# Where a row block's statistics and a shared bank's copies are computed: five tiles moved to VectorE, six copies to ScalarE

## The chip, the cores and the metric

The kernel runs on one core of a Trainium2 chip. The metric is the device time of one execution in microseconds. The kernel before was run five times; its median is 1464.83 us (1460.11 to 1469.95).

## The reference

The reference is an adaptive-layernorm block. A vector c gives six modulation rows; x goes through a layernorm with modulation and a recurrent attention over segments of 32 tokens, and then through a shifted mixer with an MLP. The change touches only the second half of the mixer:

```python
        hs = jnp.concatenate([g0, g1, g2, g3], axis=-1) @ w2
        x1 = x + hs
        h2 = _gelu(_layernorm(x1, axis=-1) @ w3) @ w4
        return x1 + h2
```

Here x has 2048 rows of 1024, w2 is 1024 x 1024, w3 is 1024 x 3584 and w4 is 3584 x 1024, all in bf16. The layernorm subtracts a row's mean and divides by the root of its variance plus 1e-5.

## The kernel before, in words

The kernel first does the attention (its projections, scores and outputs take most of the span), then the mixer in three stages: w1 (lines 1225 to 1233), w2 (lines 1355 to 1386) and w3 with w4 (lines 1430 to 1588). w1's last tiles end at about 1048.5 us of the profiled execution, w2 lasts until 1104.1, and w3 and w4 take the rest.

**w2.** The 2048 rows are worked in 16 tiles of 128 rows, t0 to t15. `Ba(t)` (line 1355) loads the tile u (what is added to the product) with a DMA on SP's queue, and multiplies two halves of 512 columns by eight matmuls each (line 1366), each half in a PSUM bank of its own. VectorE adds u while it takes a half out of its bank into x1b (line 1368, an operation that also sums each row), and ScalarE's queue stores x1b to memory (line 1369). Then comes `ln_sums` (line 1340), the layernorm of the tile: VectorE makes the negative mean of the two row sums (lines 1343, 1344), ScalarE squares x1b minus the mean and sums the squares of each row (line 1346, into z, which is overwritten later), GpSimd makes the factor and the offset in three small operations (lines 1348, 1350, 1352), and ScalarE applies them, giving z in bf16 (line 1353). `Bb(t)` (line 1374) turns z by a DMA transpose, issued on SP, into z2s, where w3 reads it. `lagged` runs `Bb(t-1)` ahead of `Ba(t)`.

The order on each engine's queue is the program's, fitted by the framework's scheduler. Three things tie the tiles together. The accumulators come from eight banks in turn, but from t13 on from the four banks of `psB` alone (line 1378). The pools of z and x1b hold four tiles each, so that t15's z lies where t11's was, and writing it waits until t11's transpose has landed. And between the tiles, seven sums of w3 weights and of z (`w3_sums` and `z_sums`, all line 1292) are put on VectorE at steps 6 to 13 (line 1385); the sums of z need the transposes of t0 to t7.

**w3.** `w3_stage(pair)` (line 1430) works on half of the rows at a time, in seven groups of columns, by a Strassen-Winograd scheme with seven products per group (line 1447). In each group, for each of two halves q: the first product goes into `bank_b`, and is copied out by `snap` (lines 1407 and 1461) while the bank goes on collecting; the second goes into `bank_e`, and `join` (line 1455) adds the copy to it on VectorE, after which ScalarE applies gelu (line 1451); the third goes into `bank_d`, copied out at line 1470; the fourth is added in `bank_b`, copied out at line 1472; then the fifth, named S3 in the code, is added in `bank_b`, the sixth, S4, in `bank_d`, and the seventh in `bank_b` again. A product that adds to a bank waits until the copy of what stood there is done. The banks are opened anew for w3, over those of w2: `bank_e` and `bank_d` lie where `psB` was. The w3 loop is under `manual_schedule`, so its order is written out by hand. In the very first group (n == 0) the six copies are made by VectorE (line 1410), in the other 13 by ScalarE (line 1412). Then w4 (`w4_stage`) follows, and both again for the second half of the rows.

Of the kernel before, what the change touches and what calls it, by code (L numbers as in the profile page):

```python
# [10 lines left out]
F32 = mybir.dt.float32  # L11
F16 = mybir.dt.float16
I32 = mybir.dt.int32
ACT = mybir.ActivationFunctionType
ALU = mybir.AluOpType
# [4 lines left out]
P = 128  # L20
# [9 lines left out]
NTT = S // P  # L30
# [30 lines left out]
def kernel(ctx, tc, A_x, A_mem0, A_Wq, A_Wk, A_Wv, A_Wo, A_seg_len, B_x, B_w1, B_w2, B_w3, B_w4, c, w_mod, out,  # L61
           dbg=None, force_fallback=False, no_fallback=False):
    nc = tc.nc
# [106 lines left out]
    def first_pass(late_hook):  # L170
# [6 lines left out]
        def acc_tile():  # L177
            acc_ctr[0] += 1
            return acc_pools[acc_ctr[0] % len(acc_pools)].tile([P, 512], F32, name="acc")
# [335 lines left out]
        for p in range(2):  # L515
# [3 lines left out]
            s1 = nc.vector.tensor_tensor(S1, A21, A22, ALU.add)  # L519
# [534 lines left out]
        bsm = LT.enter_context(tc.tile_pool(name="x1_sm", bufs=8))  # L1054
# [65 lines left out]
        ln = {}  # L1120

        def ln_stats(t, halves, rstd):
            stt = bsm.tile([P, 2, 6], F32, name="ln_st")
            for i in range(2):
                nc.vector.bn_stats(out=stt[:, i, :], in_=halves[i])
            mv = bsm.tile([P, 2], F32, name="ln_mv")
            nc.vector.bn_aggr(out=mv[:], in_=stt[:])
            nc.vector.tensor_scalar(mv[:, 1:2], mv[:, 1:2], EPS, None, ALU.add)
            nc.vector.tensor_scalar(mv[:, 0:1], mv[:, 0:1], -1.0, None, ALU.mult)
            nmr = bsm.tile([P, 1], F32, name="ln_nmr")  # L1130
            nc.gpsimd.tensor_tensor(rstd, mv[:, 1:2], mhalf[:], ALU.pow)
            nc.gpsimd.tensor_tensor(nmr[:], mv[:, 0:1], rstd, ALU.mult)
            ln[t] = nmr[:], rstd

        def halves_of(ap):
            return [ap[:, n * 512:(n + 1) * 512] for n in range(2)]
# [62 lines left out]
        U1, sums1, _ = wave(1)  # L1199
# [109 lines left out]
        def load_upto(n):  # L1309
            while ring_ctr[0] <= min(n, 21):  # L1310
                ring_load(ring_ctr[0])
                ring_ctr[0] += 1
# [25 lines left out]
        bsm = LT2.enter_context(tc.tile_pool(name="x2_sm", bufs=8))  # L1338

        def ln_sums(smp, dst, src, sums):  # L1340

            nm = smp.tile([P, 1], F32, name="ln_nm")
            nc.vector.tensor_tensor(nm[:], sums[:, 0:1], sums[:, 1:2], ALU.add)
            nc.vector.tensor_scalar(nm[:], nm[:], -1.0 / D, None, ALU.mult)
            sq = smp.tile([P, 1], F32, name="ln_sq")
            nc.scalar.activation(dst, src, ACT.Square, bias=nm[:], accum_out=sq[:])
            ve = smp.tile([P, 1], F32, name="ln_ve")
            nc.gpsimd.tensor_scalar(ve[:], sq[:], 1.0 / D, EPS, ALU.mult, ALU.add)
            rstd = smp.tile([P, 1], F32, name="ln_rstd")
            nc.gpsimd.tensor_tensor(rstd[:], ve[:], mhalf[:], ALU.pow)  # L1350
            nmr = smp.tile([P, 1], F32, name="ln_nmr")
            nc.gpsimd.tensor_tensor(nmr[:], nm[:], rstd[:], ALU.mult)
            nc.scalar.activation(dst, src, ACT.Identity, bias=nmr[:], scale=rstd[:])

        def Ba(t):
            def f():
                ts = slice(t * P, (t + 1) * P)
                u = tu.tile([P, D], BF16, name="u2")
                nc.sync.dma_start(u[:], u_d[ts, :])
                x1b = tp.tile([P, D], F32, name="x1b")  # L1360
                sums = bsm.tile([P, 2], F32, name="ln_sums")
                for n2 in range(2):
                    acc = acc_tile()
                    for kt in range(KT):
                        o = 2 + t * P + SHIFT[kt]
                        nc.tensor.matmul(acc[:], lhsT=h1Ts[kt // 4][:, kt % 4, o:o + P], rhs=w2s[0][:, kt, n2 * 512:(n2 + 1) * 512], start=(kt == 0), stop=(kt == KT - 1))  # L1366
                    cs = slice(n2 * 512, (n2 + 1) * 512)
                    nc.vector.scalar_tensor_tensor(x1b[:, cs], acc[:], 1.0, u[:, cs], ALU.mult, ALU.add, accum_out=sums[:, n2:n2 + 1])
                nc.scalar.dma_start(x1b_d[ts, :], x1b[:])
                zs[t] = z = tz.tile([P, D], BF16, name="z")  # L1370
                ln_sums(bsm, z[:], x1b[:], sums)
            return f

        def Bb(t):
# [24 lines left out]
        stA = RF.enter_context(tc.tile_pool(name="x3_sA", bufs=4, side="right"))  # L1399
        st2 = RF.enter_context(tc.tile_pool(name="x3_s2", bufs=2, side="right"))  # L1400
# [3 lines left out]
        pse = RF.enter_context(tc.tile_pool(name="ps_e", bufs=2, space=PSUM))  # L1404
        psd = RF.enter_context(tc.tile_pool(name="ps_d", bufs=2, space=PSUM))

        def snap(pool, src, on_dve=False):
            s = pool.tile([P, 512], F32, name="snap")
            if on_dve:
                nc.vector.tensor_copy(s[:], src[:])  # L1410
            else:
                nc.scalar.copy(s[:], src[:])  # L1412
            return s

        def addend_units(pair):

            def mk(t, n):
                def f():
                    rows, cs = slice(t * P, (t + 1) * P), slice(n * 512, (n + 1) * 512)
                    xb = rsq.tile([P, 512], F32, name="xb3")  # L1420
                    nc.sync.dma_start(xb[:], x1b_d[rows, cs])
                    x1 = rsq.tile([P, 512], F32, name="x13")
                    nc.sync.dma_start(x1[:], x1_d[rows, cs])
                    nc.gpsimd.tensor_tensor(xb[:], xb[:], gb_b[:, cs], ALU.mult)
                    nc.gpsimd.tensor_tensor(x1[:], xb[:], x1[:], ALU.add)
                    nc.gpsimd.dma_start(rs_d[rows, cs], x1[:])
                return f
            return [mk(t, n) for t in range(pair * 8, pair * 8 + 8) for n in range(2)]

        def w3_stage(pair):  # L1430

            hq = [[hq_p.tile([P, 14, 512], BF16, name=f"hq{a}{f}") for f in range(2)] for a in range(2)]
            A11, A12, S4, A22, S1, S2, S3 = zsum[pair]
            add = addend_units(pair)
            for g in range(7):
                n = pair * 11 + g
                load_upto(n + 2)
                B11, B21, B22, T4, T1, T2, T3 = ready[n]  # L1440
                st = [{} for _ in range(2)]

                def prod(bank, A, B, start):
                    for q in range(2):
                        acc = st[q][bank]
                        for k in range(4):
                            nc.tensor.matmul(acc[:], lhsT=B[:, k, q * P:(q + 1) * P], rhs=A[:, k, :], start=(start and k == 0), stop=(k == 3), skip_group_check=True)  # L1447
                        yield q

                def gelu(a, f, q, src):  # L1450
                    nc.scalar.activation(hq[a][f][:, g * 2 + q, :], src[:], ACT.Gelu_apprx_tanh)  # L1451

                def join(a, f, q, bank, s):
                    t = stm.tile([P, 512], F32, name="join")
                    nc.vector.tensor_tensor(t[:], st[q][bank][:], st[q][s][:], ALU.add)  # L1455
                    gelu(a, f, q, t)

                for q in range(2):
                    st[q]["b"] = psb.tile([P, 512], F32, name="bank_b")
                for q in prod("b", A11, B11, True):  # L1460
                    st[q]["s1"] = snap(stA, st[q]["b"], n == 0)
                for q in range(2):
                    st[q]["e"] = pse.tile([P, 512], F32, name="bank_e")
                for q in prod("e", A12, B21, True):
                    join(0, 0, q, "e", "s1")
                dve(T4, B21, T2, ALU.subtract)
                for q in range(2):
                    st[q]["d"] = psd.tile([P, 512], F32, name="bank_d")
                for q in prod("d", S1, T1, True):
                    st[q]["s5"] = snap(stA, st[q]["d"], n == 0)  # L1470
                for q in prod("b", S2, T2, False):
                    st[q]["s2"] = snap(st2, st[q]["b"], n == 0)
                for q in prod("b", S3, T3, False):
                    join(1, 1, q, "b", "s5")
                for q in prod("d", S4, B22, False):
                    join(0, 1, q, "d", "s2")
                for q in prod("b", A22, T4, False):
                    gelu(1, 0, q, st[q]["b"])
                for u in w3_sums(n + 1) if g < 6 else []:
                    u()  # L1480
                for u in add[16 * g // 7:16 * (g + 1) // 7]:
                    u()
            return hq
# [805 lines left out]
```

## Time and profile before

| What | Value |
|---|---|
| median of five runs | 1464.83 us |
| the profiled execution | 1464.35 us |
| its span, first to last instruction | 1462.6 us |
| TensorE (PE) busy | 1397.9 us, 96% |
| VectorE (DVE) busy | 971.3 us, 66% |
| ScalarE (ACT) busy | 692.1 us, 47% |
| GpSimd (POOL) busy | 480.3 us, 33% |
| mean granted TensorE clock | 0.992 |
| chain that ended last, by engine | TensorE 73%, VectorE 10%, DMA 9%, ScalarE 4% |

How to read it: times are those of one execution. A line of a timeline has the start in us from the span's start, the time it took, the engine, the line of the kernel, the operation, what it wrote and read, the shapes, how many instructions were merged into the line, and in brackets how long the engine sat idle just before and what ended that. In a table of stretches each row has the stretch, its length, and the busy time and count of TensorE's matmuls and weight loads, VectorE, ScalarE and GpSimd; the last three columns are the granted clock as a share of full speed, the busy share of the DMA engines and what they moved in GB/s. Of merged matmuls the time runs to the modelled end of the last one, so neighbours overlap a little; a product of eight matmuls follows the one before at 1.73 us.

### The profile page before, as it was taken

To read this page: it belongs to the slowest core of one execution; us is meant where nothing else is said; L and a number is where in the kernel's file an instruction comes from. 1 tells how busy PE (TensorE), PEld (TensorE's weight loads), DVE (VectorE), ACT (ScalarE), POOL (GpSimd) and SP (SyncE) were. 2 spreads that over 40 slices of the span, in tenths; PEclk is the share of its full clock that TensorE was granted. 3 is DMA by queue.
4 is the path that set the end of the run, shared out by engine and by line. 5 is a ranking of instruction groups with operands and counts; after the bars stand their busy time and mean duration, and the time that the engine had idled before them with its cause. 6 is when DMAs were issued, how large, how long until landed. Compare 5 with 4: busy or idle time off the path is not lost.

```text
span 1462.6 us, 24721 instructions
## 1 busy us (share of the span) xinstructions
PE 1397.9 (96%) x9080; PEld 741.4 (51%) x9126; DVE 971.3 (66%) x1995; ACT 692.1 (47%) x1473; POOL 480.3 (33%) x661
## 2 busy tenths in 40 slices
PE   6999999999999999999999999999797999999998
PEld 4665555555555555555555444444343444444443
DVE  6627777777776778777754648887255667566684
ACT  3635566465665656566664013326365650056400
POOL 6120321514122202220001025555124663546625
PEclk9999999999999999999999999999999999999999
DMA  9778978878787776787749999969499783477812
GB/s 336 271 227 197 183 169 201 210 162 211 177 196 201 171 173 162 182 201 182 161 135 315 356 374 288 309 189 262 137 273 224 237 280 109 151 230 250 283 40 79
DMA packets 389237, 310.69 MB, mean 212 GB/s; under 512 B 199658, under 2 KB 336874, under 8 KB 385266
## 3 DMA queue, kind: packets, MB, share of 16 engines
q1 hardware_dynamic: 356576, 244.03, 62.0%
q0 software_dynamic: 13856, 46.16, 9.0%
q10 hardware_dynamic: 18674, 18.83, 4.3%
q8 instruction: 73, 1.20, 0.3%
q14 instruction: 58, 0.48, 0.1%
HBM read 199.38 MB, written 59.02 MB: 177 GB/s over the span
## 4 chain that ended last, share of the span: by engine, by line
PE 73%; DVE 10%; DMA 9%; ACT 4%; issue 3%; POOL 1%; SPq 0%; ACTq 0%; DVEq 0%; POOLq 0%
PE acc L649 26%; PE acc L987 9%; PE bank_b L1498 7%; PE bank_b L1447 6%; PE acc L323 3%; PE bank_d L1447 3%; DMA s<-OTw_d 3%; PE bank_e L1498 2%; PE bank_d L1498 2%; PE acc L333 2%; PE acc L1366 2%; PE ps_o L774 2%; DMA wk<-in_A_Wk_dram 2%; PE ps_s L757 2%; PE bank_e L1447 1%
## 5 line engine op out<-in xcount | busy, mean ns | idle before, releaser
L649 PEld LDWEIGHTS <-T 128*128 128x128 f16 x1408 | 130.7, 98 | 124.6 <-issue 9.9
L617 ACT COPY snap<-acc 128x480 f32<-128x480 f32 x264 | 146.0, 565 | 91.3 <-PE acc L649 81.3
L987 PE MATMUL acc<-wstream,s 128*128 128x512 f16 (+1 forms) x855 | 187.0, 379 | 1.7 <-DMA wstream<-in_A_Wo_dram 0.6
L649 PE MATMUL acc<-hs,T 128*128 128x480 f16 x704 | 160.5, 367 | 5.1 <-DVE QT L621 2.9
L649 PE MATMUL acc<-hh,T 128*128 128x480 bf16 (+1 forms) x704 | 163.8, 368 | 1.1 <-DVE KT L621 0.9
L987 PEld LDWEIGHTS <-s 128*128 128x128 f16 (+1 forms) x864 | 84.3, 98 | 103.9 <-DVE s L1002 1.8
L1447 PEld LDWEIGHTS <-ring 128*128 128x128 f16 (+1 forms) x784 | 77.0, 98 | 104.9 <-issue 13.3
L799 POOL DMA_DIRECT2D OTw_d<-OT x32 | 24.7, 773 | 264.0 <-DMA OT<-O 217.4
L761 ACT ACTIVATE E<-ps_s 99x495 bf16<-99x495 f32 (+2 forms) x160 | 88.0, 550 | 41.4 <-PE ps_s L757 41.0
L649 PE MATMUL acc<-hh,wq 128*128 128x480 bf16 x464 | 105.5, 365 | 0.0
L781 DVE TENSOR_TENSOR O<-ps_o,rin_all 99x384 bf16<-99x384 f32 (+1 forms) x192 | 97.2, 510 | 3.9
L621 DVE TENSOR_TENSOR KT<-acc,snap 128x480 bf16<-128x480 f32 x116 | 74.4, 654 | 24.2 <-PE acc L649 17.7
L774 PE MATMUL ps_o<-V,E 99*128 99x129 bf16 (+1 forms) x704 | 81.4, 220 | 8.6 <-DVE O L781 3.0
L1412 ACT COPY snap<-bank_b 128x512 f32<-128x512 f32 x68 | 39.6, 586 | 105.3 <-PE bank_b L1498 58.2
L1498 PEld LDWEIGHTS <-hq 128*128 128x128 bf16 (+1 forms) x560 | 54.8, 98 | 66.1
L763 DVE TENSOR_TENSOR E<-E,maskB 99x495 bf16<-99x495 bf16 (+1 forms) x128 | 53.7, 419 | 47.9 <-ACT E L761 46.2
L774 PEld LDWEIGHTS <-E 99*128 99x128 bf16 (+1 forms) x704 | 57.3, 98 | 46.0 <-DVE O L781 4.8
L1292 DVE TENSOR_TENSOR ring<-ring 128x1024 f16<-128x1024 bf16 (+1 forms) x64 | 76.3, 1211 | 5.7 <-PE bank_b L1498 5.2
L779 ACT ACTIVATE O<-ps_o,rin_all 99x128 bf16<-99x128 f32 x192 | 56.7, 370 | 42.6 <-DVE rin_all L776 39.3
L1451 ACT ACTIVATE hq<-join 128x512 bf16<-128x512 f32 x84 | 52.8, 630 | 45.1 <-DVE join L1455 45.1
L621 DVE TENSOR_TENSOR VT<-acc,snap 128x480 bf16<-128x480 f32 x90 | 58.1, 652 | 22.8 <-PE acc L649 15.8
L1498 PE MATMUL bank_b<-ring,hq 128*128 128x512 f16 (+1 forms) x334 | 73.1, 379 | 0.1
(266 smaller groups left out, 2682.8 us busy)
## 6 DMA issues: line engine op xcount, KB each, us to landing
OTw_d<-OT POOLq DMA_DIRECT2D x32, 512.0 KB, 6.2
wstream<-WoT_d SPq DMA_DIRECT2D x16, 1024.0 KB, 8.8
wstream<-in_B_w_dram SPq DMA_DIRECT2D x28, 512.0 KB, 5.0
ring<-in_B_w_dram SPq DMA_DIRECT2D x28, 512.0 KB, 5.4
ring<-in_B_w_dram SPq DMA_DIRECT2D x8, 1792.0 KB, 10.3
s<-OTw_d SPq DMA_DIRECT2D x13, 1024.0 KB, 8.1
wstream<-in_A_Wo_dram SPq DMA_DIRECT2D x11, 1024.0 KB, 11.2
wq<-in_A_Wq_dram SPq DMA_DIRECT2D x16, 512.0 KB, 5.8
```

Of the source, the lines that this page charges most:

```text
L617: nc.scalar.copy(t[:], st[q][bank][:, 0:CH])
L621: nc.vector.tensor_tensor(view(d, i), chunks(st[q][bank]), chunks(st[q][s_]), ALU.add)
L649: nc.tensor.matmul(acc[:, 0:CH], lhsT=B[:, k, :], rhs=A[:, k, :], start=(j in (1, 2, 5) and k == 0), stop=(k == 3), skip_group_check=True)
L761: nc.scalar.activation(E[:rows, 0:o], ps[:rows, 0:o], ACT.Exp, scale=DH ** -0.5)
L763: nc.vector.tensor_tensor(E[:rows, 0:o], E[:rows, 0:o], mk[:rows, 0:o], ALU.mult)
L774: nc.tensor.matmul(ps[:, i, :], lhsT=state["e", h, t // 5][:k, c:c + P], rhs=V[:k, t, 0:DH + 1], start=True, stop=True)
L779: nc.scalar.mul(O[:rows, t, :], ps[:rows, i, 0:DH], rin[:, i:i + 1])
L781: nc.vector.tensor_tensor(O[:rows, ts[0]:ts[0] + n, :], ps[:rows, 0:n, 0:DH], rin[:, :, None].to_broadcast([rows, n, DH]), ALU.mult)
L987: nc.tensor.matmul(acc[:], lhsT=A[:, k, i * P:(i + 1) * P], rhs=B[:, k, :], start=(j in (1, 2, 5) and hf == 0 and k == 0), stop=(hf == 1 a ...
L1292: return nc.vector.tensor_tensor(dst, a, b, op)
L1447: nc.tensor.matmul(acc[:], lhsT=B[:, k, q * P:(q + 1) * P], rhs=A[:, k, :], start=(start and k == 0), stop=(k == 3), skip_group_check=True)
L1498: nc.tensor.matmul(acc[:], lhsT=L3[:, k, i * P:(i + 1) * P], rhs=R3[:, k, :], start=(start and k == 0), stop=(k == 13), skip_group_check=True)
```

## The change

For five tiles, t9, t11, t13, t14 and t15, the row statistics are made by VectorE. It adds u with a plain addition, without row sums, and then makes the statistics with `ln_stats`, the helper that an earlier stage uses: a statistics pass over each half of x1b, their aggregation, two small steps, and the power and the product on GpSimd. ScalarE's Square goes for these tiles. The Identity that gives z stays on ScalarE for t9, t11, t13 and t14; for t15 VectorE computes z as one operation with a factor and an offset per row. The other eleven tiles are as they were. And the six copies of w3's first group are made by ScalarE, as in all other groups.

```diff
+        BY_STATS = (9, 11, 13, 14, 15)
+
         def Ba(t):
...
                     cs = slice(n2 * 512, (n2 + 1) * 512)
-                    nc.vector.scalar_tensor_tensor(x1b[:, cs], acc[:], 1.0, u[:, cs], ALU.mult, ALU.add, accum_out=sums[:, n2:n2 + 1])
+                    if t in BY_STATS:
+                        nc.vector.tensor_tensor(x1b[:, cs], acc[:], u[:, cs], ALU.add)
+                    else:
+                        nc.vector.scalar_tensor_tensor(x1b[:, cs], acc[:], 1.0, u[:, cs], ALU.mult, ALU.add, accum_out=sums[:, n2:n2 + 1])
                 nc.scalar.dma_start(x1b_d[ts, :], x1b[:])
                 zs[t] = z = tz.tile([P, D], BF16, name="z")
-                ln_sums(bsm, z[:], x1b[:], sums)
+                if t in BY_STATS:
+                    rstd = bsm.tile([P, 1], F32, name="ln_rstd")
+                    ln_stats(t, halves_of(x1b[:]), rstd[:])
+                    nmr, _ = ln[t]
+                    if t == NTT - 1:
+                        nc.vector.tensor_scalar(z[:], x1b[:], rstd[:], nmr, ALU.mult, ALU.add)
+                    else:
+                        nc.scalar.activation(z[:], x1b[:], ACT.Identity, bias=nmr, scale=rstd[:])
+                else:
+                    ln_sums(bsm, z[:], x1b[:], sums)
...
-        def snap(pool, src, on_dve=False):
+        def snap(pool, src):
             s = pool.tile([P, 512], F32, name="snap")
-            if on_dve:
-                nc.vector.tensor_copy(s[:], src[:])
-            else:
-                nc.scalar.copy(s[:], src[:])
+            nc.scalar.copy(s[:], src[:])
             return s
...
-                    st[q]["s1"] = snap(stA, st[q]["b"], n == 0)
+                    st[q]["s1"] = snap(stA, st[q]["b"])
...
-                    st[q]["s5"] = snap(stA, st[q]["d"], n == 0)
+                    st[q]["s5"] = snap(stA, st[q]["d"])
...
-                    st[q]["s2"] = snap(st2, st[q]["b"], n == 0)
+                    st[q]["s2"] = snap(st2, st[q]["b"])
```

`ln_stats`, which the five tiles now call, stands at line 1122 of the kernel before and is not changed:

```python
        def ln_stats(t, halves, rstd):
            stt = bsm.tile([P, 2, 6], F32, name="ln_st")
            for i in range(2):
                nc.vector.bn_stats(out=stt[:, i, :], in_=halves[i])
            mv = bsm.tile([P, 2], F32, name="ln_mv")
            nc.vector.bn_aggr(out=mv[:], in_=stt[:])
            nc.vector.tensor_scalar(mv[:, 1:2], mv[:, 1:2], EPS, None, ALU.add)
            nc.vector.tensor_scalar(mv[:, 0:1], mv[:, 0:1], -1.0, None, ALU.mult)
            nmr = bsm.tile([P, 1], F32, name="ln_nmr")
            nc.gpsimd.tensor_tensor(rstd, mv[:, 1:2], mhalf[:], ALU.pow)
            nc.gpsimd.tensor_tensor(nmr[:], mv[:, 0:1], rstd, ALU.mult)
            ln[t] = nmr[:], rstd
```

## The prediction

> **What bounds the kernel now.** I read the page first: TensorE is 96% busy over a span of 1462.6 us, so a change to other engines can only win what TensorE still waits for. I then asked for TensorE's timeline from the w2 stage (tiles t0 to t15, one row block each) to the end. It has three gaps there, of 7.34, 1.52 and 1.55 us; the first is in the place that the change touches.
>
> ```profile
> 1107.57 1.89 PE L1447 MATMUL bank_d<-zs,ring 128*128 128x512 f16 x8
> 1109.30 1.89 PE L1447 MATMUL bank_b<-zs,ring 128*128 128x512 f16 x8
> 1118.53 3.41 PE L1447 MATMUL bank_b<-zs,ring 128*128 128x512 f16 x8 [7.34 <-DVE snap L1410]
> 1121.77 1.89 PE L1447 MATMUL bank_d<-zs,ring 128*128 128x512 f16 x8
> ```
>
> TensorE stands 7.34 us in w3's first group, and then takes 3.41 us for eight matmuls that take 1.89 us in the rows around. From its start to the next row they use 3.24 us where the others use 1.73: 1.51 us more. The table of stretches gives the reason, the granted clock in its third column from the end:
>
> ```profile
> 1111.20:1118.50 7.30, 0.00 (x0) 0.00 (x0) 3.71 (x7) 3.57 (x5) 0.93 (x3) 0.75 0.75 150
> 1118.50:1121.70 3.20, 3.17 (x8) 1.17 (x8) 1.26 (x2) 0.55 (x1) 1.54 (x2) 0.51 0.89 288
> ```
>
> The stall therefore costs 7.34 + 1.51 = 8.85 us, and that is the ceiling of what can be won here. VectorE's timeline shows what it waited for:
>
> ```profile
> 1105.10 0.69 DVE L1368 SCALAR_TENSOR_TENSOR x1b<-acc,u 128x512 f32<-128x512 f32 x1
> 1106.63 0.68 DVE L1410 COPY snap<-bank_b 128x512 f32<-128x512 f32 x1
> 1114.79 1.29 DVE L1455 TENSOR_TENSOR join<-bank_e,snap 128x512 f32<-128x512 f32 x2 [7.47 <-ACT z L1353]
> 1117.79 1.28 DVE L1410 COPY snap<-bank_b 128x512 f32<-128x512 f32 x2
> ```
>
> The first join needs memory that t15's last ScalarE pass still reads; the four snaps of banks d and b are queued behind that join, and TensorE needs the last pair. ScalarE is late by its own period:
>
> ```profile
> 1107.48 1.15 ACT L1346 ACTIVATE z<-x1b,ln_nm 128x1024 bf16<-128x1024 f32 x1
> 1111.08 1.13 ACT L1346 ACTIVATE z<-x1b,ln_nm 128x1024 bf16<-128x1024 f32 x1
> 1113.52 1.24 ACT L1353 ACTIVATE z<-x1b,ln_nmr,ln_rstd 128x1024 bf16<-128x1024 f32 x1 [1.21 <-POOL ln_nmr L1352]
> ```
>
> Square, GpSimd's three small steps and the Identity repeat every 3.6 us, TensorE's 16 matmuls every 3.455 us; with hiccups around 1092 to 1099 ScalarE ends t15 at 1114.76, when TensorE left w2 at 1104.12.
>
> **What the Trainium skill says.** "TensorE: Matmul & The Clock Gate", What's actually happening: the clock halves after an idle window of about 3.4 us. The trace agrees: clock 0.51 after 7.34 us idle, no loss after the two gaps of 1.5 us at 1289 and 1292. "VectorE: DVE Perf Modes", The perf-mode tier table and The TRN2 errata: an fp32 scalar operation within SBUF handles two elements a cycle, one with a second tensor or PSUM one, and fp32 adds take (N+151)/0.96 ns. The trace: 692 ns for the 512-wide join (formula 691), 517 ns for L1073's 704 wide f32 to bf16 (at two a cycle 524). No run here has t15's new VectorE pass.
>
> **The change, part by part.** Durations are the profile's; the waits of both programs are in their built form. I roll the order of the changed program forward from 1081.9, when t9 is evacuated.
>
> *Squares off ScalarE.* Five Squares go (1.13 + 0.19 us each, 6.6 us in all), and t15's Identity too. ScalarE is off the path for t9 to t13 then.
>
> *Statistics on VectorE.* Per such tile: two 512-wide statistics passes (684 ns, 0.60 us apart from a neighbour, 0.73 us when the pass waits for the one before it), an aggregation and two small steps. From first evacuation to mv this is 0.73 + 0.60 + 0.73 + 0.72 + 0.25 + 0.07 + 0.07 = 3.17 us, against 1.67 us before (1095.52 to 1097.19): 1.50 us more per tile. For t9 it hides in VectorE's waits for TensorE (0.6 and 1.0 us twice per tile). After that VectorE waits for the transpose of t7, ended at 1091.38, and the four z sums (1.13 us each) stand between the tiles; from there on VectorE has no gap left but 1.6 us. So:
> t11 evacuated from 1092.71 (as before), z sum 1095.88; t12 from 1097.01, sum 1098.68; t13 from 1099.81, sum 1102.98; t14 from 1104.11 and 1104.71, its statistics 1105.31 to 1106.6; t15 from 1106.52, its second half, behind t14's small steps, at 1108.0 to 1108.69. Before, that ended at 1105.79: 2.9 us later.
>
> *New wait.* Bank e's first matmul waits for just that evacuation (the same wait existed and cost nothing at 1105.85). TensorE stands there from 1105.85 to 1108.75, 2.9 us, with all of w3 queued behind it. t15's own matmuls wait for t13's evacuation, done 1100.5 and 1101.8 against 1100.7 and 1102.4: free, by 0.2 us.
>
> *t15's z on VectorE.* Second statistics 1108.73, mv 1109.91, GpSimd's two steps (0.56 + 0.19 + gaps) 1110.76, z at 1110.79. Its price is between 0.55 (L423, 1024 bf16 wide, 546 ns) and 1.22 us (1024 at one a cycle, by the page's formula); I take 0.69 us, two a cycle ((512+151)/0.96, an estimate of that page). The join starts at 1111.5.
>
> *Snaps on ScalarE.* Six copies (585 ns, 0.5 us apart) leave VectorE. Those of bank b come behind t14's Identity (needs mv of t14, 1108.08, and GpSimd; 1108.96 to 1110.20), so 1110.10 to 1111.2; needed by TensorE at 1112.2, free by 1 us. Those of banks d and b stand behind the two gelus of the join. The second pair's first group has the very order: join at 1289.32, TensorE's S3 product at 1292.77, 3.45 us. Here 1111.5 + 3.45 = 1114.95. TensorE is through with e, d and S2 at 1108.75 + 3 x 1.73 = 1113.93, so it waits 1.0 us more.
>
> *Moved.* GpSimd now does t11's power before t10's product, so t10's Identity goes from 1094.50 to 1096.8; its next user, t14's evacuation, comes at 1104.1: free. On SP's queue t9's transpose now precedes the loads of u for t14 and t15, which also wait for later evacuations: issued 1094.8 and 1098.4 for 1094.04 and 1096.85. With the longest landing seen (7.5 us) u of t15 is there at 1105.9, wanted at 1106.5. The x1b store of t15 precedes the snaps on ScalarE, but is issued before t14's Identity ends.
>
> *Sum.* The S4 product, after S3, starts at 1114.95 + 1.73 = 1116.68 against 1121.77: **5.1 us won**. Behind it TensorE has no gap until 1287.7, and the two there are made by output DMAs queued on ScalarE relative to TensorE's own pace; so the shift reaches the end. If 2.9 us idle do lower the clock, e, d and S2 end at 1115.6, half hidden behind the 1.0 us: 0.7 us lost. The profiled execution took 1464.35 us with its span of 1462.6 and 1.75 around it; it goes to 1459.3. It lies 0.48 below the median of 1464.83, which goes to **1459.7**.
>
> **Rivals.**
> *All is won.* If VectorE kept its pace, both gaps and the slow clock would go: 1464.83 - 8.85 = 1456.0. For it: VectorE is only 66% busy over the span. Against: its chain from 1091.4 on is work after work, 17.3 us of it against TensorE's 14.4.
> *VectorE is later still.* The chain starts at a DMA landing (t7's transpose, 6.2 us; such transposes took 3.1 to 10.0) that was free until now and is passed on one to one. Two to three us there, or 1.22 us for z, leave 2 us: 1462.8.
> *Slower.* t15's z takes the buffer of t11's z, so on VectorE it waits until t11's transpose has landed, and the joins with it. That transpose is issued behind u of t15 and t10's, near 1101.3; with the median of 5.8 us it lands at 1107.1, with the longest at 1111.3, wanted at 1110.8. Each us beyond is a us of the end; at 1110.8 + 5.1 = 1115.9 the gain is gone. DMA engines are 98% busy in w2, so at 1118 the kernel takes 1464.8 + 2.1 = 1466.9.
> That the squares don't leave ScalarE is excluded: the built program has eleven.
>
> **Numbers.** Forecast 0.58 (its own range 1458 to 1461.5), all won 0.12, VectorE later 0.23, slower 0.07. Half a per cent (7.3 us, below 1457.5 or above 1472.2) is about what a measurement of this kernel can tell from no change. Faster by more: most of the second case and the lower edge of the first, as single runs scatter from 1460.1 to 1470.0: 0.19. Slower by more: the tail of the last, 0.04. Within: 0.77. The range 1455.5 to 1465.5 takes in the first three.
>
> **What would show it.** TensorE's gap in w3 splits: about 2.9 us ahead of bank e, put down to the evacuation, and about 1 us ahead of the S3 product, put down to a ScalarE snap; granted clock near 1.0 throughout; t15's second evacuation ends near 1108.7; z on VectorE 0.69 us. Wrong: if the gap ahead of e is missing (then all is won), if VectorE waits for a DMA ahead of t15's u or z (slower), if a third gap comes later in w3.

## The result, and the profile after

The changed kernel takes 1459.87 us (median of 42 executions, 1454.27 to 1486.0) against 1463.86 of the kernel before beside it (79 executions). The ratio is 0.9971, with a 95% interval of 0.996 to 0.9982: 4.2 us faster, between 2.6 and 5.9. A second set (22 executions) gave 1459.1 us and 0.9964 (0.9944 to 0.9984). Here and below the ratio and what is worked out from it leave out executions in a slower state, the medians do not. The forecast was 1459.7.

The profiled execution after took 1463.18 us with a span of 1461.4. That its span is only 1.2 us shorter than before says little: w3 starts at 1106.96 us here and at 1104.12 before, and none of these 2.84 us is the change's. w1 already begins 1.55 us later (982.25 against 980.70), 1.29 us come in w1, where TensorE's two waits for transposes fell differently, and w2 takes TensorE 55.27 us in both. A second profiled execution of the changed kernel starts w3 at 1104.15. So I measure from w3's first matmul on, in every kernel below, and write such times with a plus sign.

TensorE's timeline of the changed kernel:

```profile
1106.96 1.89 PE L1458 MATMUL bank_b<-z2a,ring 128*128 128x512 bf16 x8
1111.51 3.15 PE L1458 MATMUL bank_e<-z2a,ring 128*128 128x512 bf16 x8 [2.66 <-DVE x1b L1371]
1114.45 2.36 PE L1458 MATMUL bank_d<-zs,ring 128*128 128x512 f16 x8
1116.64 3.62 PE L1458 MATMUL bank_b<-zs,ring 128*128 128x512 f16 x16
1120.10 1.89 PE L1458 MATMUL bank_d<-zs,ring 128*128 128x512 f16 x8
...
1131.00 1.89 PE L1458 MATMUL bank_b<-zs,ring 128*128 128x512 f16 x8 [0.38 <-ACT snap L1423]
```

The gap of 7.34 us ahead of S3 is gone. In its place stands 2.66 us ahead of bank e, put down to t15's evacuation. S2 and S3 run as one row of 16, so no gap is left between them. S4 starts at +13.14 us (1120.10 less 1106.96), before at +17.65 (1121.77 less 1104.12): 4.51 us won in this stage. A small gap of 0.38 us is new in the next group. The matmuls of e and d are slow, and the table of stretches says why:

```profile
1108.80:1111.50 2.70, 0.05 (x1) 0.00 (x0) 2.67 (x9) 0.18 (x1) 0.55 (x1) 1.00 0.92 160
1111.50:1114.40 2.90, 2.89 (x8) 1.05 (x8) 1.92 (x5) 2.20 (x3) 0.93 (x3) 0.58 1.19 297
1114.40:1116.60 2.20, 2.20 (x9) 0.94 (x8) 1.89 (x3) 1.32 (x3) 0.00 (x0) 0.77 1.11 316
```

After the 2.66 us the granted clock is 0.58, then 0.77. VectorE is busy for 2.67 us of the gap's 2.70: it is the engine that TensorE waits for. Its timeline:

```profile
1110.77 0.68 DVE L1371 TENSOR_TENSOR x1b<-acc,u 128x512 f32<-128x512 f32 x1
1113.55 0.81 DVE L1381 TENSOR_SCALAR z<-x1b,ln_rstd,ln_nmr 128x1024 bf16<-128x1024 f32 x1 [0.87 <-POOL ln_nmr L1132]
1114.49 1.29 DVE L1466 TENSOR_TENSOR join<-bank_e,snap 128x512 f32<-128x512 f32 x2
```

t15's second half begins to leave its bank at +3.81, z follows at +6.59, the first join at +7.53 (before: +10.67).

### The profile page after: what moved, and what is told of

The parts are those of the page before. It is cut to its first block, busy times and chain, and to the rows that moved or that the text cites. A ratio compares the mean times of both kernels' runs of the same rounds, so it can differ in the third digit from the quotient of the medians.

```text
span 1461.4 us, 24707 instructions
## 1 busy us (share of the span) xinstructions
PE 1401.0 (96%) x9080; PEld 741.9 (51%) x9126; DVE 984.4 (67%) x1995; ACT 689.0 (47%) x1468; POOL 483.2 (33%) x656
## 4 chain that ended last, share of the span: by engine, by line
PE 75%; DVE 10%; DMA 7%; ACT 3%; issue 2%; POOL 1%; SPq 0%; DVEq 0%; ACTq 0%; POOLq 0%
PE acc L649 27%; PE acc L987 9%; PE bank_b L1509 7%; PE bank_b L1458 6%; PE acc L323 3%; PE bank_d L1458 3%; DMA s<-OTw_d 3%; PE acc L1368 3%; PE bank_e L1509 2%; PE bank_d L1509 2%; PE acc L333 2%; DMA wk<-in_A_Wk_dram 2%; PE ps_o L774 2%; PE bank_e L1458 2%; PE ps_s L757 2%
## 5 line engine op out<-in xcount | busy, mean ns | idle before, releaser
L1292 DVE TENSOR_TENSOR ring<-ring 128x1024 f16<-128x1024 bf16 (+1 forms) x64 | 82.6, 1309 | 5.7 <-PE bank_b L1509 5.2
L621 DVE TENSOR_TENSOR VT<-acc,snap 128x480 bf16<-128x480 f32 x90 | 58.2, 652 | 22.8 <-PE acc L649 15.8
```

What stands on the lines that cost most here:

```text
L621: nc.vector.tensor_tensor(view(d, i), chunks(st[q][bank]), chunks(st[q][s_]), ALU.add)
L1292: return nc.vector.tensor_tensor(dst, a, b, op)
```

## The experiments

Each was compared with the kernel before in the same set of runs. The four columns of distances are worked out from TensorE's timeline of one profiled execution: from w3's first matmul to S4's first, to w4's first, to the first of the second half of the rows, and to the end of the span. What an edit costs in w2 lies ahead of that mark and is not in them: TensorE takes 55.3 us for w2, but 55.5 in e4 and e12, 55.9 in e9 and 57.0 in e6.

| Kernel | ratio to before (95%) | S4 | w4 | second half | end |
|---|---|---|---|---|---|
| before | 1 | +17.65 | +93.75 | +178.35 | +358.48 |
| changed | 0.9971 (0.996 to 0.9982) | +13.14 | +89.78 | +174.39 | +354.44 |
| changed, again | 0.9964 (0.9944 to 0.9984) | +12.93 | +89.16 | +173.77 | +353.65 |
| e1 statistics only | 0.9958 (0.9939 to 0.9977) | +13.66 | +90.30 | +174.91 | +354.88 |
| e2 snaps only | 0.9999 (0.9981 to 1.0017) | +20.84 | +97.80 | +182.41 | +362.25 |
| e3 other memory, before | 1.0016 (0.9998 to 1.0034) | +8.96 | +86.20 | +183.97 | +363.75 |
| e4 other memory, changed | 0.9967 (0.995 to 0.9984) | +12.58 | +90.53 | +175.99 | +356.10 |
| e5 z15 on ScalarE | 0.9961 (0.9939 to 0.9983) | +13.14 | +89.60 | +174.21 | +353.81 |
| e6 four tiles | 0.996 (0.994 to 0.998) | +12.09 | +89.28 | +173.88 | +353.60 |
| e7 e3 and more buffers | 0.9973 (0.996 to 0.9986) | +8.71 | +86.38 | +170.99 | +352.53 |
| e8 more buffers, before | 1.0052 (1.0028 to 1.0075) | +18.02 | +97.26 | +181.86 | +364.91 |
| e9 e3, two tiles, early weights | 1.0037 (1.0016 to 1.0059) | +8.73 | +85.29 | +179.03 | +358.83 |
| e11 e3, early weights | 1.0022 (0.9996 to 1.0048) | +8.75 | +86.70 | +180.25 | +359.87 |
| e12 three tiles | 0.9973 (0.9956 to 0.999) | +13.90 | +90.49 | +175.10 | +355.13 |

My theory: before, the first join waited for memory that t15's last ScalarE pass held; the change ends that pass's hold early, and VectorE's own queue now sets the end. Rivals: the move of the snaps is what won; or ScalarE's lateness holds w3 up in more ways than by that memory.

**e1 and e2: each half of the change alone.** In e1 the snaps of the first group stay on VectorE; e2 is the kernel before with the snaps moved.

```diff
-                    st[q]["s1"] = snap(stA, st[q]["b"])
+                    st[q]["s1"] = snap(stA, st[q]["b"], n == 0)
```

> The changed kernel with w3's first six snaps on VectorE as before; the statistics and t15's z as changed. Theory (VectorE's own queue now sets the end): two bank-b snaps of 0.6 us fall between t15's second statistics and its z, so z15 and the first join come 1.2 us later than in the changed kernel, and the S3 product comes 3.7 us behind the join, as in the kernel before. A gap of about 1 us appears ahead of S3; the gap of 2.7 us ahead of bank e stays. About 1.0 us slower than the changed kernel, about 3.0 faster than before. Rival (the move of the snaps is what won): the gap ahead of S3 is 4 us or more and the time is within 1 us of the kernel before.

TensorE in e1:

```profile
1107.55 3.47 PE L1461 MATMUL bank_e<-z2a,ring 128*128 128x512 bf16 x8 [2.44 <-DVE x1b L1371]
...
1115.16 1.89 PE L1461 MATMUL bank_b<-zs,ring 128*128 128x512 f16 x8 [0.69 <-DVE snap L1424]
```

The two gaps are where they were expected, the second 0.69 us. In the stage e1 is 0.5 us behind the changed kernel; its time cannot be told from it.

> The kernel before with only the six snaps moved to ScalarE; the squares of t9 to t15 stay on ScalarE. Theory: the second bank-b snap and all that follows stand behind t15's Identity on ScalarE, which ends at 1114.8; S2's second half waits for it (gap ahead of S2 instead of S3) and S3 still starts near 1118.5. Between 1 us faster and 0.5 us slower than before. Rival (the move of the snaps is what won): 3 to 4 us faster than before.

The snaps alone win nothing (0.9999). In the profiled execution S2 waits twice, for snaps that stand behind t15's Square and its Identity on ScalarE, and ScalarE itself had waited:

```profile
1117.51 1.86 PE L1447 MATMUL bank_b<-zs,ring 128*128 128x512 f16 x4 [6.37 <-ACT snap L1412]
1119.97 1.86 PE L1447 MATMUL bank_b<-zs,ring 128*128 128x512 f16 x4 [0.59 <-ACT snap L1412]
```

```profile
1112.17 1.15 ACT L1346 ACTIVATE z<-x1b,ln_nm 128x1024 bf16<-128x1024 f32 x1 [3.40 <-DMA z2b<-z]
```

The last row is t14's Square, which writes into the buffer of t10's z and so waits until that was transposed: 3.40 us in this execution, and S3 comes 3.1 us later than before. The changed kernel writes t14's z only by its Identity, later. The statistics, not the snaps, make the gain.

**e3 and e4: other memory, no operation moved.** The pools of joins and snaps are opened ahead of the others (their lines further down go), and so get other memory; e3 starts from the kernel before, e4 from the changed one.

```diff
+        stm = RF.enter_context(tc.tile_pool(name="x3_sm", bufs=3, side="right"))
+        stA = RF.enter_context(tc.tile_pool(name="x3_sA", bufs=4, side="right"))
+        st2 = RF.enter_context(tc.tile_pool(name="x3_s2", bufs=2, side="right"))
         hq_p = RF.enter_context(tc.tile_pool(name="x3_h", bufs=1, side="right"))
```

> The kernel before with no operation moved: only the pools of the joins and snaps get other memory, which t15's last pass does not read, so that the first join waits for nothing of ScalarE. Theory A (the stall was a wait for memory): S3's gap of 7.3 us and its slow matmuls vanish, 8 to 8.9 us faster than before, about 4.5 faster than the changed kernel. Theory B (ScalarE's lateness itself holds w3 up, by its gelus behind t15's Identity): within 2 us of before, as the gap moves to a later product.

Both theories were half right. w3's first group has no gap at all: S4 starts at +8.96, and five products of 1.73 us are 8.65. The first join no longer waits for t15's last ScalarE pass; it comes 8.1 us ahead of it. VectorE, then ScalarE, in e3:

```profile
1106.42 1.27 DVE L1455 TENSOR_TENSOR join<-bank_e,snap 128x512 f32<-128x512 f32 x2
```

```profile
1114.55 1.24 ACT L1353 ACTIVATE z<-x1b,ln_nmr,ln_rstd 128x1024 bf16<-128x1024 f32 x1 [0.70 <-POOL ln_nmr L1352]
```

So the stall before was that wait for memory and nothing else. Yet the time is no shorter, for w4 stalls. TensorE, then VectorE, in e3:

```profile
1219.34 8.11 PE L1498 MATMUL bank_e<-ring,zs 128*128 128x512 f16 x28 [5.75 <-DVE join L1520]
...
1237.11 7.77 PE L1498 MATMUL bank_e<-ring,hq 128*128 128x512 bf16 x28 [3.62 <-DVE hq L1292]
```

```profile
1214.79 3.89 DVE L1292 TENSOR_TENSOR ring<-ring 128x7168 f16<-128x7168 bf16 x1 [15.64 <-DMA ring<-in_B_w_dram]
...
1222.67 1.73 DVE L1524 TENSOR_TENSOR o<-join,rs 128x512 bf16<-128x512 f32 x1 [2.19 <-POOL rs L1518]
```

VectorE waits 15.64 us for w4's weights and then for the addends (what is added to the output: loaded on SP, worked by GpSimd, stored, and loaded again in w4). On SP's queue these loads stand behind t15's transpose; in e3 the first is issued at +15.8 us, before at +12.1. Of these 3.7 us, 2.1 are the transpose itself (+12.8, before +10.7): in this execution t14's Square waited 1.99 us for t10's transpose.

Another 1.25 us come from the edit. It moved no operation of an engine, but the pools that are opened after the moved ones come to lie elsewhere too, and, it seems with them, one load moved: in the kernel before three of w3's weight blocks are loaded ahead of w2, in e3 two, and the third block's two loads stand between t15's transpose and the first addend load. SP's queue in e3:

```profile
1117.59 1.15 SPq L1303 DMA_DIRECT2D ring<-in_B_w_dram  x2
1118.84 1.01 SPq L1421 DMA_DIRECT2D xb<-x1b_d  x1
```

The same is so in e4, e7, e9 and e11. So what w4 loses in them can't be put down to an earlier w3 alone.

> The changed kernel with the same other memory for joins and snaps. Theory: in the changed kernel the first join stands behind t15's z in VectorE's own queue, and bank e waits for t15's evacuation, so memory is no longer what is waited for: within 0.5 us of the changed kernel, the gap of 2.7 us ahead of bank e unchanged. Rival (memory is still waited for): 2 us or more faster than the changed kernel.

TensorE in e4:

```profile
1101.24 1.89 PE L1458 MATMUL bank_e<-z2a,ring 128*128 128x512 bf16 x8 [2.75 <-DVE x1b L1371]
...
1107.46 1.89 PE L1458 MATMUL bank_b<-zs,ring 128*128 128x512 f16 x8 [0.88 <-ACT snap L1423]
```

As expected: the gap ahead of bank e stays, 2.75 us, and the time is the changed kernel's (0.9967 against 0.9971). In this execution the matmuls behind the gap run at full speed (1.89 us), and so the second gap that I had forecast, about 1 us ahead of S3 for a ScalarE snap, is there with 0.88 us; S4 starts at +12.58, forecast +12.56 (1116.68 less 1104.12). From there e4 falls behind: ahead of the changed kernel by 0.56 us at S4, it starts the second half 1.60 us later, with gaps of 0.25, 0.72 and 0.45 us in later groups of w3 and of 0.50 in w4.

**e11, e9, e7, e8: what w4 waits for.** e11 is e3 with w4's third weight block loaded one group earlier; e9 adds to that the statistics of t9 and t11.

```diff
-                load_upto(n + 2)
+                load_upto(n + (3 if g == 6 else 2))
```

> e3 (other memory for joins and snaps, nothing else moved) with only the third w4 weight block loaded one group earlier, ahead of the last three addend loads on SP. Theory (VectorE's 15.6 us wait for weights in e3 was SP's queue, not the transfer): that wait falls below 4 us and w4's gap of 5.8 us ahead of its third product vanishes; the addends themselves stay late, so the gap of 3.6 us in the next product stays or grows to 6. 3 to 6 us faster than e3. Rival (the transfer itself is slow): the wait stays above 10 us and the time is that of e3.

> The other memory of e3 for joins and snaps, statistics on VectorE for t9 and t11 only (first snaps on VectorE, t15's z on ScalarE as in the kernel before), and the third w4 weight block of each pair loaded one group earlier, ahead of the last three addend loads on SP. Theory: the joins don't wait for t15; VectorE is not late, as t9's statistics are hidden and t11's take the place of its wait for u of t15; ScalarE is through with t15 about 2.6 us earlier than before (two squares fewer), so SP reaches the addends about 3 us earlier and w4 does not wait, or under 2 us. S4 starts 9 us after w3's first matmul (17.6 before, 13.1 in the changed kernel): 6.5 to 8 us faster than before, ratio near 0.995. Rival (w4 gives it back as in e3): gaps of 5 us or more in w4, within 3 us of before.

In e11 the wait for weights is gone, and the addends take its place, 6.01 us; e9 shows the same, 6.22 us. TensorE and VectorE in e9:

```profile
1231.01 0.61 PE L1512 MATMUL bank_e<-ring,hq 128*128 128x512 bf16 x1 [6.22 <-DVE hq L1292]
```

```profile
1216.57 1.74 DVE L1538 TENSOR_TENSOR o<-join,rs 128x512 bf16<-128x512 f32 x1 [6.16 <-POOL rs L1532]
```

My expectation for e9 failed: t15's z was not early, and the first addend load was issued at +14.4, not near +9. GpSimd waits 9.96 us for one of the last addend loads; that the early weight load holds it up is likely, but not shown. In e7 the addends' buffers go from two to four, with e3's memory; e8 is the kernel before with that alone.

```diff
-        rsq = RF.enter_context(tc.tile_pool(name="x3_rq", bufs=2, side="right"))
+        rsq = RF.enter_context(tc.tile_pool(name="x3_rq", bufs=4, side="right"))
```

> The kernel before with the other memory of e3 for joins and snaps, and four buffers in place of two for the addends' loads. Theory (in e3 the gain of w3's first group was given back in w4, where VectorE waited for weights and addends queued on SP behind addend loads without a free buffer): both gaps in w4 (5.8 and 3.6 us in e3) vanish or shrink below 1 us in sum, and the 8 us won in w3 reach the end: 7 to 8.5 us faster than before, ratio near 0.995. Rival (w4 waits for the transfers themselves, the DMA engines being full): the gaps stay above 5 us in sum and the time is that of e3.

> Control: the kernel before with only the addends' buffers raised from two to four. Theory: nothing waits for them in the kernel before (no gap in w4), so within 0.5 us of before. Rival: 2 us or more faster, which would mean that e7's gain is not that of w3's first group.

e7 has neither gap in w4 and reaches the second half at +170.99, 7.4 us ahead of before: the gain of w3's first group does arrive if the addends are in time. But it ends only 6.0 us ahead in the profile and 3.9 in the medians, and the control says why: four buffers alone cost 7.6 us (1.0052). Against e8, which has the same buffers, e7's S4 is 9.3 us and its end 12.4 us earlier. VectorE, then GpSimd, in e8:

```profile
1151.96 4.88 DVE L1292 TENSOR_TENSOR ring<-ring 128x1024 f16<-128x1024 bf16 x3
```

```profile
1152.48 1.60 POOL L1425 TENSOR_TENSOR x<-xb,x 128x512 f32<-128x512 f32 x1
...
1154.99 1.28 POOL L1424 TENSOR_TENSOR xb<-xb,gb_b 128x512 f32<-128x512 f32 x1
```

Three weight sums take 4.88 us while GpSimd adds beside them, 2.01 us in e3's first group without it; between 1125 and 1190 us one takes 1360 ns on average in e8 and 856 before. The joins come late, and TensorE waits 0.2 to 1.1 us in many groups. The Trainium skill ("SBUF — State Buffer", SBUF: two separate sides) says that an operation of VectorE with two SBUF inputs and one of GpSimd lock each other out for a whole instruction. The durations agree, and GpSimd's power, in the last section, shows such a wait on its own.

Set side by side from the timelines of SP and GpSimd, for each kernel the time of the first addend load from w3's start, and of the last addend's store from w4's start: before +12.1 and +6.2, changed +10.2 and +11.1, e4 +10.8 and +14.0 (0.5 us of gaps in w4), e3 +15.8 and +21.1 (9.4 us), e11 +14.1 and +22.7 (6.2 us), e9 +14.4 and +23.2 (6.4 us). What the addends have is the time from their first load to w4's start: 81.7 us before, 79.6 in the changed kernel, 79.8 in e4, 72.6 in e11, 70.9 in e9, 70.4 in e3. e2 fits: its first load comes as late as +15.4, but it has 82.4 us and no gap in w4. This time is not all: e4 has as much as the changed kernel, and its last store comes 2.9 us later. In kernels without a gap in w4 the last store came at +11.4 at the latest (e6), with gaps from +14.0 on (e4); the limit lies between.

**e5, e6, e12: the parts of VectorE's queue.** e5 leaves t15's z on ScalarE; e6 and e12 shorten the list of tiles.

```diff
-        BY_STATS = (9, 11, 13, 14, 15)
+        BY_STATS = (9, 11, 13, 15)
```

> The changed kernel with t15's z computed by ScalarE's Identity instead of VectorE. Theory: the Identity (1.2 us) starts when GpSimd's product is there, as VectorE's pass did, and w3's two bank-b snaps stand behind it on ScalarE; the first join waits for the first of these snaps and comes about 1 us later than in the changed kernel, and S3 with it: 0.5 to 1 us slower than the changed kernel. Rival (z on VectorE is what won most): back within 1 us of the kernel before.

The join stands 3.84 us behind bank e's start (2.98 in the changed kernel), so z on ScalarE does cost 0.9 us there; but bank e came 0.4 us earlier in this execution and S4 starts at the same +13.14. The time cannot be told from the changed kernel's.

> The changed kernel with t14 taken out of the list of statistics tiles (its squares on ScalarE again). Theory (each statistics tile costs VectorE 1.5 us, passed on one to one to the gap ahead of bank e): that gap goes from 2.7 to about 1.2 us, the first join and t15's z come 1.5 us earlier, S4 starts about 11.2 us after w3's first matmul (13.1 in the changed kernel), and 1.5 us are won against the changed kernel. Rival (the gap is set by u of t15 or by t15's own statistics): the gap stays within 0.5 us of 2.7.

TensorE in e6:

```profile
1102.55 3.61 PE L1368 MATMUL acc<-s,s 128*128 128x512 bf16 x16 [1.55 <-DVE x1b L1371]
1106.00 1.89 PE L1458 MATMUL bank_b<-z2a,ring 128*128 128x512 bf16 x8
1109.93 1.89 PE L1458 MATMUL bank_e<-z2a,ring 128*128 128x512 bf16 x8 [2.04 <-DVE x1b L1371]
```

Here VectorE's chain began later (it waited 5.22 us for t7's transpose, 3.42 in the changed kernel), and TensorE waits for it already ahead of t15, in w2. That w2 takes 1.7 us longer is more than the 1.05 us by which S4's +12.09 is ahead of the changed kernel. From the first sum of z to t15's second evacuation VectorE takes 15.61 us, 16.31 in the changed kernel: t14's statistics cost 0.70 us, not 1.5.

> The changed kernel with t13 and t14 taken out of the list of statistics tiles (t9, t11 and t15 stay; t15's z and the first snaps as in the changed kernel). Theory: VectorE is 1.5 us earlier again than with four tiles, so the gap ahead of bank e shrinks to about 0.5 us, the first join comes 1.5 us earlier, S4 starts about 10.7 us after w3's first matmul (12.1 with four tiles, 13.1 in the changed kernel); the last addend store comes about 12 to 13 us after w4's start, just ahead of where e4 began to lose: 2 to 2.5 us faster than the changed kernel, 6 to 6.5 faster than before, ratio near 0.9957. Rival (the second bound in w4 gives it back): gaps of 1 us or more in w4, no gain against the changed kernel.

e12's diff is that of e6 with (9, 11, 15). The same stretch takes 14.14 us, 1.47 less than with t13. Bank e's gap shrinks to 0.56 us as expected, but ScalarE takes over. TensorE and ScalarE in e12:

```profile
1118.92 1.89 PE L1458 MATMUL bank_e<-z2a,ring 128*128 128x512 bf16 x8 [0.56 <-DVE x1b L1371]
1120.65 1.89 PE L1458 MATMUL bank_d<-zs,ring 128*128 128x512 f16 x8
1125.22 1.89 PE L1458 MATMUL bank_b<-zs,ring 128*128 128x512 f16 x8 [2.68 <-ACT snap L1423]
1128.65 1.89 PE L1458 MATMUL bank_b<-zs,ring 128*128 128x512 f16 x8 [1.55 <-ACT snap L1423]
```

```profile
1123.46 1.24 ACT L1353 ACTIVATE z<-x1b,ln_nmr,ln_rstd 128x1024 bf16<-128x1024 f32 x1 [1.62 <-POOL ln_nmr L1352]
1124.60 1.05 ACT L1423 COPY snap<-bank_b 128x512 f32<-128x512 f32 x2
```

With Squares for t13 and t14, bank b's snaps come behind t14's Identity at +8.1 us and S2 waits 2.68 us for them. I had not expected that: S4 comes at +13.90 in place of 10.7, and the ratio is 0.9973 in place of 0.9957. Few tiles make ScalarE late, many make VectorE late.

**The changed kernel again.**

> The changed kernel once more, on the chip of e9 and e11, to compare e9 with it: ratio to before 0.996 to 0.998; the gap of 2 to 3 us ahead of bank e, S4 12.5 to 13.2 us after w3's first matmul; whether the matmuls behind that gap run at full clock or not is open, as both were seen after gaps of 2.2 to 2.75 us.

S4 at +12.93 and a gap of 2.69 us; e's matmuls are slow, d's are not. None of these kernels is shown to be faster than the changed one: the ratios of e1, e5 and e6 are lower, but their intervals overlap its own.

## Why the prediction was right, point by point

- **The stall and its cause** were right, and e3 proves them: with other memory and no operation moved, S4 starts 8.69 us earlier, nearly all of 7.34 and 1.51.
- **The squares, the statistics and the new wait** were right: t15's second evacuation at +3.81 (forecast +3.88), a gap of 2.66 us ahead of bank e (forecast 2.9). The price of 1.50 us a tile holds for t13 (1.47), and is 0.70 for t14, whose steps lie between t15's.
- **t15's z** took 0.81 us where I took 0.69, within the bounds of 0.55 and 1.22. It then set the join at +7.53 (forecast +7.38).
- **The gap of 1 us ahead of S3 did not come, and the clock did fall.** I took the clock to stay at full speed and named its fall as a further 0.7 us. The profile before could have told: its clock fell behind gaps of 2.65 us (at 118.64) and 2.44 (at 284.61), and stayed behind another of 2.44 (at 1010.92). Here it fell: e and d took 2.94 and 2.19 us from start to start in place of 1.73, 1.67 us more. This ate the 1 us for which S3 would have waited and pushed S3 to +11.4 (forecast +10.8). 4.51 us were won where I had 5.1; the mis-sized term is the clock, put at nothing in the sum and worth 0.6 us. Where the clock stayed up, in e4, the gap ahead of S3 and S4's start are those of the forecast.
- **The number 1459.7** was met to 0.2 us, and that is luck in part. The gain was 4.0 us between the medians (4.2 by the ratio) where I had 5.1, but the kernel before measured 1463.86 beside it and not the 1464.83 from which I had subtracted.
- **"The shift reaches the end"** was right for this change and for a reason I did not see. Of 4.51 us 4.04 are left at the end; the rest goes with the new gap of 0.38 us, where GpSimd's adds now meet more of VectorE's weight sums (three in 4.93 us; 3.40 before). But the last addend's store moved from 6.2 to 11.1 us after w4's start; with it at 14.0 e4 has 0.5 us of gaps in w4, with it beyond 21 e3, e9 and e11 have 6 and more. It helps that t15's z, and with it SP's queue, is earlier (first addend load +10.2, +12.1 before).
- **The rivals.** "All is won" did not happen, as VectorE's chain is work after work. In e3 the full gain in this stage was lost in w4, but with a weight load in the addends' way; what would be left without that load is not shown. "VectorE is later still": t7's transpose landed as before in this execution; in e6 VectorE waited 1.8 us longer for it (5.22 against 3.42). "Slower": t15's z on VectorE waited for GpSimd in the runs that I read (0.87 us; 3.50 in e12), never for t11's transpose.

## What to carry to other kernels

A wait named after a compute engine can be a wait for the memory that its last pass still reads: other memory for the waiting tile shows it in one run. Look then at what else the new layout moved: here it was one weight load on another queue, and the next stage stalled. Before a stall is priced as a gain, follow the queues behind it to the next stage and measure how late each may come there; here 4 us passed, and 8 passed only with more buffers for the addends (e7). When work is moved between two engines that both feed the bound one, the best share should lie where both are just in time; with three, four and five tiles the runs show the two kinds of lateness, but no difference in time that is clear of the noise.

## What the runs showed of the hardware that I had not expected

- Gaps of 2.2 to 3.0 us on TensorE halve the clock in some executions and not in others. Over the 14 profiled executions, from 60 us on, it fell behind 26 of 45 such gaps (fell: 2.23 to 2.96 us, stayed: 2.26 to 2.85), also behind gaps of one place in the program and one length: in w1 behind 2.47 us it fell in e7, e8 and the changed kernel and stayed in e9. It fell behind all 23 gaps of 3.62 us and more. Of 117 gaps of 0.9 to 2.1 us at full clock it fell behind one alone, of 1.08 us in e8, where TensorE stood another 0.77 us after a single matmul. Behind the gap of 2.66 us in the changed kernel the first three matmuls still start 0.215 us apart, and from the fourth on 0.427. The skill's page on TensorE ("TensorE: Matmul & The Clock Gate", What's actually happening) states an idle window of about 3.4 us that runs freely; the free running fits the scatter, the 3.4 us do not.
- GpSimd's power on 128 x 1 values takes 0.55 us, but longer where it starts during certain operations of VectorE: 0.98 to 0.99 us beside an operation on two bf16 tensors in SBUF (0.68 us), 1.52 to 1.58 beside a sum of z (1.21), 2.6 beside a larger one of 2.28 us, and 0.82 beside one with a single input, f32 to bf16 (0.52). In all 22 such cases of the kernels before and after it ended 0.41 to 0.43 us after VectorE's operation. Beside statistics passes and beside operations that read a PSUM bank it took 0.54 to 0.57 us. GpSimd in the changed kernel, beside a sum of z that runs from 1098.74 to 1099.96:

```profile
1098.84 1.52 POOL L1131 TENSOR_TENSOR ln_rstd<-ln_mv,mhalf 128x1 f32<-128x1 f32 x1 [4.64 <-DVE ln_mv L1129]
```
